# Batch 0 by casting loads with interleaved transposes and dummies, weight sums between products, two score steps in the first matmul

## The chip, the cores and the metric

One core of one Trainium2 chip runs the kernel. The metric is the device time in microseconds (us), the median of several executions. A profile is one such execution; its span is about 2 us shorter than the time of the same run. A ratio is the mean time of one kernel's fast runs over that of the other's in the same rounds, so it is not quite the ratio of the medians that are quoted. Times inside a kernel come from single profiles; heads that are the same instruction for instruction differ by about 1 us there, so differences below that are not read as effects.

Engines are named as in the profile: PE is TensorE (matmuls) and PEld its weight loads, DVE is VectorE, ACT is ScalarE, POOL is GpSimd, SP is SyncE, which issues DMAs; a q behind the name (SPq, POOLq) marks its DMA issues. L92 is line 92 of that kernel's file. `att` (three pairs of banks) and `ffp` (two banks) are the tiles in PSUM, the memory that matmuls write. The granted clock is the share of its full clock that PE was given. A casting DMA changes f32 to f16 on the way; a dummy is a matmul whose result nobody reads.

## The reference, cut to what matters

```python
# q, k, v: 8 batches x 12 heads x 448 x 64 f32;  w_in 768 x 2048, w_out 2048 x 768
scores = q @ k.T / sqrt(64) - log(448)
attn = sigmoid(scores) @ v                 # per head
x = attn, heads joined to 768 columns      # 3584 tokens
h = x @ w_in
out = (h * sigmoid(h)) @ w_out
```

q and k are drawn with a deviation of 0.1, so the scores before the shift have a deviation near 0.01 against a shift of -6.1. The comparison with the reference therefore hardly sees an error in q or k.

## The kernel before: the parts that matter

Heads are taken four at a time (a "quad", three to a batch; quads 0 to 2 are batch 0, quads 3 to 5 batch 1). A quad has seven score steps (four matmuls of 64x64 by 448 and one sigmoid of 128x896 each) and one set of values (28 matmuls), which gives a third of xT. Per batch: `ff1`, the first matmul (96 matmuls and a sigmoid product, giving gT), then `ff2_pair`, the second matmul (called the second product below), in seven products of eight matmuls (a Strassen form that needs four sums of w_out, once, and four sums `gs` of gT for each pair). The score steps of the next batch are interleaved with the second product of this one.

```python
    def load(kind, b, n):                     # f32, hardware queue (SP), 5 buffers
        ...
    def cast(kind, b, n):                     # f32 to f16 on GpSimd, q, k and v
        ...
    # batch 0, in front of everything
    for n in range(NQ):
        for kind in range(2):
            load(kind, 0, n)
            cast(kind, 0, n)
            pe_transpose(kind, 0, n, kind, "act" if kind else "dve")
        load(2, 0, n)
        cast(2, 0, n)
        ...                                   # w_in, w_out pieces by casting DMAs (GpSimd)
        us = [("s", 0, n, r) for r in range(R)]
        if n > 0:
            us.insert(2, ("a", 0, n - 1))     # values of the quad before
        while us:
            visit(us[:3])                     # three PSUM pairs
            us = us[3:]
    visit([("a", 0, NQ - 1)])
    for i in range(NQ, NQ + 3):               # batch 1: load, cast, DMA transpose
        prep(i)
        stage(i)
    w_out_sums()                              # four sums of 128x3072 on DVE

    for b in range(B):
        ff1(b)
        ...                                   # ff2 of b between the score steps of b + 1

    def ff2_pair(m):
        nc.vector.tensor_add(gs[:, 0], a21, a22)
        nc.vector.tensor_sub(gs[:, 1], gs[:, 0], a11)
        nc.vector.tensor_sub(gs[:, 3], a12, gs[:, 1])
        nc.vector.tensor_sub(gs[:, 2], a11, a21)
        ...
        yield from prod(X, a11, B11, True, False)
        copy(0, X)                            # snap copy, DVE, behind all four gs
        yield from prod(Z, s1, T1, True, False)
        copy(1, Z)
        yield from prod(X, s2, T2, False, False)
        ...
```

Of the kernel before, what the change touches and what calls it, by code (L numbers as in the profile page):

```python
# [16 lines left out]
def kernel(  # L17
# [9 lines left out]
    nc = tc.nc  # L27
# [34 lines left out]
    NSLOT = 14  # L62
    attnT = sb("attnT", [P, 2 * NSLOT, S])
    tsig = [sb(f"tsig{i}", [P, 2, S]) for i in range(2)]
    st32 = [sb(f"st32_{i}", [P, 2, S], F32) for i in range(5)]
    st16 = [sb(f"st16_{i}", [P, R, 2, D]) for i in range(4)]
    v16 = [sb(f"v16_{i}", [P, 2, R, D]) for i in range(3)]
# [3 lines left out]

    att = [psum.tile([P, 2, 512], F32, tag=f"att{i}", name=f"att{i}") for i in range(3)]
    ffp = [psum.tile([P, 512], F32, tag=f"ffp{i}", name=f"ffp{i}") for i in range(2)]

    nc.vector.memset(warm, 0.0)
    nc.gpsimd.memset(bias_s, NEG_LOG_S)
    make_identity(nc, ident)


    B11 = lambda fc: w_out_sb[:, fc, 0:EH]  # L80
    B21 = lambda fc: w_out_sb[:, KH + fc, 0:EH]
    B22 = lambda fc: w_out_sb[:, KH + fc, EH:]
    B12A = w_out_sb[:, 0:KH, EH:]
    T1 = lambda fc: wt[:, 0, fc, :]
    T2 = lambda fc: wt[:, 1, fc, :]
    T4N = lambda fc: wt[:, 2, fc, :]
    T3 = lambda fc: w_out_sb[:, fc, EH:]

    def w_out_sums():
        b11, b21, b22 = w_out_sb[:, 0:KH, 0:EH], w_out_sb[:, KH:, 0:EH], w_out_sb[:, KH:, EH:]  # L90
        nc.vector.tensor_sub(wt[:, 0], B12A, b11)
        nc.vector.tensor_sub(wt[:, 1], b22, wt[:, 0])  # L92
        nc.vector.tensor_sub(wt[:, 2], b21, wt[:, 1])
        nc.vector.tensor_sub(B12A, b22, B12A)


    n32 = [0]
    n16 = [0]
    staged = {}

    def load(kind, b, n):
        t = st32[n32[0] % len(st32)]
        n32[0] += 1
        src = (q, k, v)[kind]
        for g in range(2):
            h = 4 * n + 2 * g
            nc.sync.dma_start(
                t[g * HP : (g + 1) * HP],
                src[b, h : h + 2].rearrange("i (p r) d -> p i (r d)", p=HP),
            )  # L110
        staged[(kind, b, n)] = t

    def cast(kind, b, n):
        t = staged.pop((kind, b, n))
        if kind == 2:
            o = v16[(b * NQ + n) % 3]
            nc.gpsimd.tensor_copy(o.rearrange("p i r d -> p i (r d)"), t)  # L117
        else:
            o = st16[n16[0] % len(st16)]
            n16[0] += 1  # L120
            nc.gpsimd.tensor_copy(  # L121
                o.rearrange("p r i d -> p i r d"), t.rearrange("p i (r d) -> p i r d", r=R)
            )
            staged[("c", kind, b, n)] = o

    def dma_transpose(kind, b, n):
        o = staged.pop(("c", kind, b, n))
        nc.sync.dma_start_transpose(
            qkT[(b * NQ + n) % 3][kind], o.rearrange("p r i d -> p (r i d)")
        )  # L130

    def pe_transpose(kind, b, n, pair, eng):
        o = staged.pop(("c", kind, b, n))
        at = att[pair]
        for r in range(R):
            nc.tensor.matmul(
                at[:, r // 4, (r % 4) * P : (r % 4 + 1) * P],
                o[:, r].rearrange("p i d -> p (i d)"),
                ident,
                start=True,  # L140
                stop=True,
            )
        dst = qkT[(b * NQ + n) % 3][kind]
        for lo, hi, bk in ((0, 4, 0), (4, R, 1)):
            o2 = dst[:, lo:hi, :].rearrange("p r c -> p (r c)")
            i2 = at[:, bk, : (hi - lo) * P]
            if eng == "act":
                nc.scalar.copy(o2, i2)
            else:
                nc.vector.tensor_copy(o2, i2)  # L150


    def slot_of(b, n, r):
        return 2 * (((b * NQ + n) % 2) * R + r)

    def score_step(b, n, r, pair):
        qT, kT = qkT[(b * NQ + n) % 3]
        for i, j in ((0, 0), (1, 1), (0, 1), (1, 0)):
            ri = slice(i * HP, (i + 1) * HP)
            cj = slice(j * HP, (j + 1) * HP)  # L160
            nc.tensor.matmul(  # L161
                att[pair][cj, i, :S],
                kT[ri, r, cj],
                qT[ri, :, cj],
                start=True,
                stop=True,
            )

    def sigmoid(b, n, r, pair):
        s0 = slot_of(b, n, r)  # L170
        nc.scalar.activation(  # L171
            attnT[:, s0 : s0 + 2, :], att[pair][:, :, :S], AF.Sigmoid, bias=bias_s, scale=QKSCALE
        )

    def values(b, n, pair):
        vt = v16[(b * NQ + n) % 3]
        for r in range(R):
            s0 = slot_of(b, n, r)
            for i, j in ((0, 0), (1, 1), (0, 1), (1, 0)):
                rj = slice(j * HP, (j + 1) * HP)  # L180
                nc.tensor.matmul(  # L181
                    att[pair][i * HP : (i + 1) * HP, j, :S],
                    vt[rj, i, r, :],
                    attnT[rj, s0 + i, :],
                    start=(r == 0),
                    stop=(r == R - 1),
                )
        nc.vector.tensor_scalar_mul(xT[:, 2 * n : 2 * n + 2, :], att[pair][:, :, :S], SX)  # L188

    def unit_stream(b):  # L190

        o = []
        for n in range(NQ):
            for r in range(R):
                o.append(("s", b, n, r))
                if n > 0 and r == 2:
                    o.append(("a", b, n - 1))
        return o

    events = {}  # L200

    def visit(us):
        pair = 0
        for u in us:
            if u[0] == "a":
                values(u[1], u[2], pair)
                pair += 1
        for u in us:
            if u[0] == "s":
                score_step(*u[1:], pair)  # L210
                sigmoid(*u[1:], pair)
                pair += 1
        for u in us:
            for f in events.get(u, ()):
                f()

# [3 lines left out]
    def ff1(b):  # L220
        cb = (b % 2) * S
        for u in range(NFC // 2):
# [22 lines left out]
            for f in events.get(("f", b, u), ()):  # L245
                f()
# [5 lines left out]
    def ff2_pair(m):  # L252
# [6 lines left out]
        nc.vector.tensor_add(gs[:, 0], a21, a22)  # L259
        nc.vector.tensor_sub(gs[:, 1], gs[:, 0], a11)  # L260
        nc.vector.tensor_sub(gs[:, 3], a12, gs[:, 1])  # L261
        nc.vector.tensor_sub(gs[:, 2], a11, a21)  # L262
        s1, s2, s3, s4 = (gs[:, i] for i in range(4))
        x0 = nprod[0] % 2
        nprod[0] += 7
        X, Z = ffp[x0][:, :EH], ffp[1 - x0][:, :EH]
        o1, o2 = osb[nosb[0] % 3], osb[(nosb[0] + 1) % 3]
        nosb[0] += 2

        def prod(bank, a, w, first, last):  # L270
            for fc in range(KH):
# [3 lines left out]
                    w(fc),  # L275
# [17 lines left out]

        yield from prod(X, a11, B11, True, False)
        copy(0, X)
        yield from prod(Z, s1, T1, True, False)
        copy(1, Z)
        yield from prod(X, s2, T2, False, False)
        copy(2, X)
        yield from prod(Z, s4, B22, False, True)  # L300
        comb(o1[:, EH:], Z, 2)
        yield from prod(X, s3, T3, False, False)
# [7 lines left out]


    quads = [(b, n) for b in range(B) for n in range(NQ)]

    def prep(i):

        if i < len(quads):
            for kind in range(3):
                load(kind, *quads[i])
# [14 lines left out]
    def stage(i):  # L333

        if i < len(quads):
            for kind in range(3):
                cast(kind, *quads[i])
                if kind < 2:
                    dma_transpose(kind, *quads[i])


    for _ in range(10):
        nc.tensor.matmul(ffp[0], warm[:, :P], warm, start=True, stop=True)

    def at(u, f):
        events.setdefault(u, []).append(f)


    for n in range(NQ):
        for kind in range(2):  # L350
            load(kind, 0, n)
            cast(kind, 0, n)
            pe_transpose(kind, 0, n, kind, "act" if kind else "dve")
        load(2, 0, n)
        cast(2, 0, n)
        if n == 0:
            w_in_piece(0)
        if n == 1:
            w_in_piece(1)
        if n == 2:  # L360
            w_in_piece(2)
            w_in_piece(3)
            for s in range(4):
                w_out_piece(s)
        us = [("s", 0, n, r) for r in range(R)]
        if n > 0:
            us.insert(2, ("a", 0, n - 1))
        while us:
            visit(us[:3])
            us = us[3:]  # L370
    visit([("a", 0, NQ - 1)])
    for i in range(NQ, NQ + 3):
        prep(i)
        stage(i)
    w_out_sums()

    for b in range(B):
        ff1(b)
        lo, hi = (b * S) // 256, ((b + 1) * S) // 256
        mms = []  # L380
        gens = [ff2_pair(m) for m in range(lo, hi)]

        def run():
# [55 lines left out]
```

## Time and profile before

| | before |
|---|---|
| time, median of the first 3 runs | 432.3 us |
| first sigmoid | 12.3 us |
| first matmul of batch 0 starts | 45.0 us |
| second product of batch 0 starts | 81.1 us |
| first matmul of batch 1 starts | 103.7 us |
| from there to the end of the span (427.9) | 324.2 us |

The starts are those of the timeline of TensorE (PE). They cut the kernel into a head of 104 us and a steady part of 324 us. The line of the timeline that makes this cut (start, length, engine, line, what), for the kernel before:

```profile
103.65 6.59 PE L228 MATMUL att<-xT,w_in_sb 128*128 128x448 f16 x34
```

These are lines of the page's table of 40 slices (10.7 us each) for the kernel before: busy tenths of PE, the granted clock of PE in tenths, and the busy share of the DMA engines (9 stands for 90% or more).

```profile
PE   5566825989999999999999999899999999999894
...
PEclk8566675999999999999999999999999999999998
...
DMA  8999999389904995279905985699029930211022
```

The steady part is full at full clock. The first seven slices are neither. The DMA line ends at 9, so the table of stretches is needed; it gives per stretch its length, the busy time of PE, PEld, DVE, ACT and POOL (with the number of instructions), the clock, the DMA share and GB/s, for the kernel before:

```profile
20.00:30.00 10.00, 6.15 (x63) 3.24 (x62) 2.04 (x3) 6.72 (x9) 7.90 (x10) 0.67 1.17 263
30.00:40.00 10.00, 7.21 (x70) 3.82 (x69) 2.25 (x3) 6.29 (x9) 0.94 (x1) 0.67 1.22 200
...
60.00:70.00 10.00, 0.71 (x3) 0.27 (x3) 6.95 (x5) 0.67 (x1) 3.16 (x2) 0.50 1.13 193
```

From 60 to 70 us PE is busy for 0.71 us. The chain of waits (start, length, what) shows why, for the kernel before:

```profile
27.11 35.78 DMA w_out_sb<-in_moe_w_out_dram
63.01 1.77 DVE wt L92
64.81 1.76 DVE wt L93
66.56 1.67 DVE w_out_sb L94
68.23 1.01 DVE gT L244
69.29 8.94 PE att L228 x36
```

The w_out sums stand on DVE in front of the first gT products of `ff1`. They wait for the last w_out piece, which lands at 62.9 us. There are three `att` pairs, and one comes free only after its gT product, so PE stops. The list of waits of PE, longest in total first (us in total, times, longest), for the kernel before:

```profile
PE att L228 <- DVE gT L244: 12.9, 1, 12.9
PE att L161 <- ACT attnT L171: 10.0, 21, 1.7
PE att L136 <- ACT attnT L171: 3.5, 2, 2.1
PE ffp L272 <- DVE snap L283: 3.1, 7, 1.0
```

The last of these is the wait for snap copies that stand behind the four gs sums. Two of its seven times are in the last batch and cost 1.04 us each (timeline of PE).

### The profile page before, as it was taken

The numbers are of one execution on the slowest core, as the hardware profiler recorded it, in microseconds if no ns is written. First come the engines' busy times: TensorE is split into PE (matmuls) and PEld (weight loads), VectorE is DVE, ScalarE is ACT, GpSimd is POOL, SyncE is SP. The second block draws the span as 40 slices with busy tenths as digits, with TensorE's granted clock in tenths as the row PEclk, the third lists the DMA queues.
The fourth block names the chain that finished last, engine by engine and source line by source line (L and its number), as shares of the span: only waits on it lengthen the run. The fifth ranks groups of instructions, "written<-read, shape, count | busy, mean of one in ns | idle before, by whom it ended". The sixth has DMA issues, their size and how long they took to land.

```text
span 427.9 us, 7184 instructions
## 1 busy us (share of the span) xinstructions
PE 380.4 (89%) x2948; PEld 192.2 (45%) x2948; DVE 196.0 (46%) x269; ACT 222.2 (52%) x256; POOL 75.6 (18%) x87
## 2 busy tenths in 40 slices
PE   5566825989999999999999999899999999999894
PEld 2233312445545454545545554355454554455452
DVE  1121127623564445554465445344636445544652
ACT  2866102694377535872478435963677148734200
POOL 3570013122100221003100221131001200000000
PEclk8566675999999999999999999999999999999998
DMA  8999999389904995279905985699029930211022
GB/s 194 253 251 199 228 215 194 89 176 193 224 2 91 205 217 153 44 184 205 223 11 118 208 214 128 140 211 221 19 53 211 179 95 2 75 37 38 0 76 74
DMA packets 69472, 60.43 MB, mean 141 GB/s; under 512 B 42304, under 2 KB 65856, under 8 KB 69440
## 3 DMA queue, kind: packets, MB, share of 16 engines
q1 hardware_dynamic: 64192, 53.69, 57.2%
q0 software_dynamic: 5248, 6.29, 8.5%
q8 instruction: 23, 0.38, 0.4%
q14 instruction: 9, 0.07, 0.1%
HBM read 45.61 MB, written 11.01 MB: 132 GB/s over the span
## 4 chain that ended last, share of the span: by engine, by line
PE 70%; DVE 10%; DMA 9%; ACT 7%; issue 1%; POOL 1%; SPq 0%; DVEq 0%; ACTq 0%; POOLq 0%
PE att L228 24%; PE ffp L272 24%; DMA w_out_sb<-in_moe_w_out_dram 8%; PE ffp L228 8%; PE att L181 8%; ACT attnT L171 5%; PE att L161 5%; DVE gs L260 1%; DVE gs L261 1%; DVE gs L259 1%; DVE gs L262 1%; DMA st<-in_k_dram 1%; ACT tsig L239 1%; DVE snap L283 1%; DVE osb L308 1%
## 5 line engine op out<-in xcount | busy, mean ns | idle before, releaser
L171 ACT ACTIVATE attnT<-att,bias_s 128x896 f16<-128x896 f32 x168 | 156.1, 1012 | 33.4 <-PE att L161 33.1
L228 PE MATMUL att<-xT,w_in_sb 128*128 128x448 f16 x576 | 115.7, 361 | 14.2 <-DVE gT L244 12.9
L228 PEld LDWEIGHTS <-w_in_sb 128*128 128x128 f16 x768 | 76.3, 99 | 87.6 <-issue 20.2
L243 ACT ACTIVATE tsig<-att 128x896 f16<-128x896 f32 x48 | 44.0, 917 | 122.2 <-PE att L228 105.7
L244 DVE TENSOR_TENSOR gT<-att,tsig 128x896 f16<-128x896 f32 x48 | 52.3, 1091 | 70.4 <-ACT tsig L243 70.3
L121 POOL CAST st<-st 128x896 f16<-128x896 f32 x48 | 46.3, 965 | 172.5 <-DMA st<-in_q_dram 120.7
L161 PE MATMUL att<-qkT,qkT 64*64 64x448 f16 x672 | 51.8, 375 | 11.6 <-ACT attnT L171 10.0
L272 PEld LDWEIGHTS <-gs 128*128 128x128 f16 x448 | 40.4, 98 | 41.1 <-issue 16.5
L188 DVE TENSOR_SCALAR xT<-att 128x896 f16<-128x896 f32 x24 | 26.2, 1092 | 54.0 <-PE att L181 54.0
L272 PE MATMUL ffp<-wt,gs 128*128 128x384 f16 x224 | 43.0, 327 | 3.4 <-DVE snap L283 3.1
L272 PE MATMUL ffp<-w_out_sb,gT 128*128 128x384 f16 x224 | 43.4, 327 | 2.8 <-DVE gT L241 2.8
L272 PEld LDWEIGHTS <-gT 128*128 128x128 f16 x336 | 31.0, 98 | 29.5 <-issue 11.2
L181 PE MATMUL att<-attnT,v 64*64 64x448 f16 x672 | 40.4, 380 | 2.7 <-ACT attnT L171 1.7
L272 PE MATMUL ffp<-w_out_sb,gs 128*128 128x384 f16 x224 | 42.3, 327 | 0.0
L117 POOL CAST v<-st 128x896 f16<-128x896 f32 x24 | 22.5, 936 | 94.3 <-PE att L181 72.9
L228 PE MATMUL ffp<-xT,w_in_sb 128*128 128x448 f16 x192 | 38.9, 352 | 0.0
L286 DVE SCALAR_TENSOR_TENSOR osb<-ffp,snap 128x384 f32<-128x384 f32 x42 | 23.3, 555 | 33.2 <-PE ffp L272 33.2
L161 PEld LDWEIGHTS <-qkT 64*64 64x64 f16 x672 | 19.2, 108 | 41.0 <-issue 34.7
L181 PEld LDWEIGHTS <-v 64*64 64x64 f16 x672 | 20.1, 113 | 19.5 <-issue 9.7
L283 DVE TENSOR_SCALAR snap<-ffp 128x384 f32<-128x384 f32 x42 | 22.7, 553 | 11.6 <-PE ffp L272 10.9
L239 ACT ACTIVATE tsig<-ffp 128x448 f16<-128x448 f32 x32 | 17.3, 544 | 12.2 <-PE ffp L228 12.1
L241 DVE TENSOR_TENSOR gT<-ffp,tsig 128x448 f16<-128x448 f32 x32 | 19.7, 620 | 4.1 <-ACT tsig L239 4.1
(28 smaller groups left out, 105.9 us busy)
## 6 DMA issues: line engine op xcount, KB each, us to landing
st<-in_q_dram SPq DMA_DIRECT2D x48, 224.0 KB, 3.9
st<-in_k_dram SPq DMA_DIRECT2D x48, 224.0 KB, 4.8
st<-in_v_dram SPq DMA_DIRECT2D x48, 224.0 KB, 5.6
out_dram<-osb SPq DMA_DIRECT2D x56, 192.0 KB, 2.8
w_in_sb<-in_moe_w_in_dram POOLq DMA_DIRECT2D x4, 768.0 KB, 15.1
w_out_sb<-in_moe_w_out_dram POOLq DMA_DIRECT2D x4, 768.0 KB, 29.6
qkT<-st SPq DMA_TRANSPOSE x42, 3.2
```

What stands on the lines that cost most here:

```text
L117: nc.gpsimd.tensor_copy(o.rearrange("p i r d -> p i (r d)"), t)
L121: nc.gpsimd.tensor_copy(o.rearrange("p r i d -> p i r d"), t.rearrange("p i (r d) -> p i r d", r=R))
L161: nc.tensor.matmul(att[pair][cj, i, :S], kT[ri, r, cj], qT[ri, :, cj], start=True, stop=True,)
L171: nc.scalar.activation(attnT[:, s0 : s0 + 2, :], att[pair][:, :, :S], AF.Sigmoid, bias=bias_s, scale=QKSCALE)
L181: nc.tensor.matmul(att[pair][i * HP : (i + 1) * HP, j, :S], vt[rj, i, r, :], attnT[rj, s0 + i, :], start=(r == 0), stop=(r == R - 1),)
L188: nc.vector.tensor_scalar_mul(xT[:, 2 * n : 2 * n + 2, :], att[pair][:, :, :S], SX)
L228: nc.tensor.matmul(o, w_in_sb[:, cc, f * P : (f + 1) * P], xT[:, cc, :], start=(cc == 0), stop=(cc == NCC - 1),)
L243: nc.scalar.activation(ts, ph[:, :, :S], AF.Sigmoid, bias=0.0, scale=ISX)
L244: nc.vector.tensor_mul(gT[:, 2 * u : 2 * u + 2, cb : cb + S], ph[:, :, :S], ts)
L272: nc.tensor.matmul(bank, a[:, fc], w(fc), start=first and fc == 0, stop=fc == KH - 1, skip_group_check=True,)
L283: nc.vector.tensor_scalar_mul(snap[i], bank, ISX)
L286: nc.vector.scalar_tensor_tensor(o, bank, ISX, snap[i], op0=ALU.mult, op1=ALU.add)
```

## The change

Its intent: a shorter head. (1) The w_out sums go between the first pair's products, where each is needed. (2) q, k and v of batch 0 come by casting DMAs from GpSimd (only the first k comes by SP and is cast on DVE), the transposes are interleaved with the score steps, the sigmoid table is loaded at the start, and dummy matmuls fill the gaps. (3) In batches 0 and 4, whose second product is one pair only, two score steps move into the first matmul. (4) The gs sums go between products. (5) v of all batches comes by casting DMAs. The diff also moves the loads of the later quads to other points of the stream.

```diff
+    nc.scalar.activation(warm[:, 0:1], bias_s, AF.Sigmoid, bias=bias_s, scale=1.0)
...
+    load32(1, 0)
+    load16(0, 0)
+    make_identity(nc, ident)
+    nc.vector.tensor_copy(natural(0, 1), st32[1])
+    load16(1, 1)
+    load16(0, 1)
+    load16(2, 0)
+    w_in_piece(0)
...
+    dummy(14)
+    pe_transpose(1, 0, 0)
+    pe_transpose(0, 0, 1)
     for n in range(NQ):
+        for r in range(R):
+            score_step(n, r, cnt % 2)
+            sigmoid(n, r, cnt % 2)
+            cnt += 1
+            if n + 1 < NQ and r == (0 if n == 0 else 3):
+                pe_transpose(1, n + 1, 2)
+            elif n + 1 < NQ and r == (3 if n == 0 else 5):
+                pe_transpose(0, n + 1, 2)
+            elif n > 0 and r == 2:
+                value_steps(n - 1, 2, range(R))
+                to_x(n - 1, 2)
+            else:
+                dummy(2)
         if n == 0:
+            load32(1, NQ)
+            load32(0, NQ)
+            load16(2, NQ)
+            w_out_piece(0)
+            w_out_piece(1)
         if n == 1:
+            w_out_piece(2)
+            w_out_piece(3)
+            cast(1, NQ)
+            cast(0, NQ)
+            dma_transpose(1, NQ)
+            dma_transpose(0, NQ)
...
-    w_out_sums()
+    fetch(NQ + 1)
+    prepare(NQ + 1)
...
+            if u == NFC // 2 - 2 and early:      # in ff1
+                visit(early)
...
+        nc.vector.tensor_add(s1, a21, a22)       # in ff2_pair; new is m == 0
+        if new:
+            w_sum(T1, B12, B11)
         yield from prod(X, a11, B11, True, False)
         copy(0, X)
+        nc.vector.tensor_sub(s2, s1, a11)
+        if new:
+            w_sum(T2, B22, T1)
         yield from prod(Z, s1, T1, True, False)
         copy(1, Z)
+        nc.vector.tensor_sub(s4, a12, s2)
         yield from prod(X, s2, T2, False, False)
...
```

## The prediction

> **What bounds the kernel now.** The slice table shows TensorE over 95% busy from 100 to 400 us at full clock: matmul-bound. The first 104 us are not (clock 0.5 to 0.8 in most slices). The chain of waits and the timeline give this head:
> - 0 to 45.0 us: batch 0's attention. First sigmoid at 12.3 us, after serial loads, casts, transposes and a second activation-table load (1.28 us). 21 sigmoids of 0.914 us need 19.2 us; ACT pauses about 5 us at each change of quad (transposes; values of 2.83 us at half clock against 1.45).
> - 45.0 to 81.1 us: batch 0's first matmul, 18.2 us of work at full clock (as later, 103.8 to 121.9). TensorE idles from 56.4 to 69.3 us: a bank waits for a gT multiply, behind the four w_out sums (1.76 us each) on DVE, which wait for the last w_out piece (landing at 62.9 us). Then the clock is at half again.
> - 81.1 to 103.8 us: batch 0's second product with 21 score steps, ACT-bound (so is batch 4, 265 to 288).
> The DMA share is 1.1 to 1.2 from 10 to 63 us: loads are the head's second limit.
>
> **What the change does.**
> 1. The w_out sums no longer stand in front of the gT multiplies: -13 us of wait, -4 to -5 us of half-clock matmuls. All on the chain.
> 2. Interleaved transposes, early table load, casting DMAs, dummies that keep the clock up. The Trainium skill's "TensorE: Matmul & The Clock Gate", Part 1, says the clock is half until about 3.4 us of sustained activity and falls back after an idle window; this trace agrees (ten dummies 0.43 us apart, then full-clock transposes, then 0.5 in the second slice). First sigmoid near 10 us, 19.2 us of sigmoids, some 3 us of pauses, values and xT: attention ends near 34 us, not 45. -11 us.
> 3. Two score steps inside the first matmul of batches 0 and 4: each saves about 1.5 us.
> 4. gs sums between products: the last batch loses 1.04 us twice to snap copies queued behind them; with small waits elsewhere -2 to -3 us.
> 5. v by casting DMA in all batches: -22 us of GpSimd, off the path.
> Steps 1 to 3 are bounded by DMA. Estimate, from the page's queue shares (36 us of 16 engines for the weights, 245 us for the hardware queue, so about 1.84 us a load, 1.5 us a DMA transpose): 36 + nine casting loads of 1.4 + five loads + four transposes = 64 units before the last w_out piece, at 1.1 a microsecond: it lands at 55 to 60 us. The third product wants it near 58 us: little stall, at worst 5 us.
>
> **Sum.** xT of batch 0 at 34, first matmul to 52.5, second product to 75 (now 103.8): -29. Later batches -4. 432.3 - 33 = about **400 us**; 8 in 10: 393 to 409. Faster by over 2%: 0.97, within 2%: 0.02, slower: 0.01.
>
> **What would show it.** Right: the second batch's first matmul starts at 73 to 79 us; clock near 1 from 10 us; sigmoids of batch 0 nearly gapless from 10 to 32 us; GpSimd busy falls by a third. Wrong on step 1: DVE waits for w_out inside batch 0's second product and ACT idles with it. Wrong on step 2: sigmoids still pause over 2 us per quad, clock under 0.9.
>
> **What would make it wrong.** Casting loads slower than 1.4 us, or weights queued behind them, so that w_in or w_out lands late (then 405 to 412); k and q of quad 1 delayed by the next batch's loads on the same engines; the sums (7 us of DVE in batch 0's product) delaying snap copies; v landing late in the steady part.

## The result, and the profile after

The time is 406.45 us (median of 4 runs, 405.22 to 406.76) against 432.12 us (4 runs). The ratio is 0.9401, with a 95% interval of 0.9371 to 0.9431.

| | before | after | predicted |
|---|---|---|---|
| first sigmoid | 12.3 | 11.8 | 10 |
| first matmul of batch 0 starts | 45.0 | 34.4 | 34 |
| second product of batch 0 starts | 81.1 | 54.8 | 52.5 |
| first matmul of batch 1 starts | 103.7 | 84.2 | 75 |
| from there to the end | 324.2 | 320.1 | 320 |

The line of the timeline of PE that starts batch 1, for the kernel after:

```profile
84.22 6.97 PE L215 MATMUL att<-xT,w_in_sb 128*128 128x448 f16 x36
```

By length: attention of batch 0 won 10.6 us, its first matmul 15.8 us (36.1 to 20.4), and the steady part 4.2 us, but the second product of batch 0 became 6.9 us longer (22.5 to 29.5).

The same lines of the table of slices (10.1 us each), for the kernel after:

```profile
PE   6889956899999999999999998899999999999994
...
PEclk9999996999999999999999999999999999999999
...
DMA  8999987879977772767547783778178630311022
```

The clock is full at once. Slices 6 and 7 (50 to 71 us) still have a hole of PE, and the DMA engines are full no longer there. The stretches, for the kernel after:

```profile
20.00:30.00 10.00, 8.51 (x122) 3.68 (x110) 4.29 (x6) 8.12 (x9) 6.66 (x9) 1.00 1.24 206
...
50.00:60.00 10.00, 6.26 (x51) 2.56 (x49) 5.35 (x7) 8.08 (x10) 3.28 (x4) 1.00 0.89 160
60.00:70.00 10.00, 6.09 (x51) 2.69 (x52) 4.71 (x5) 1.86 (x2) 4.17 (x4) 0.66 0.79 161
```

The waits of PE, for the kernel after: the 12.9 us wait of `att` on gT is gone, and the longest is now on a DMA that fills qkT. (The second line is another wait, at the start of second products; the kernel before had it too, with 2.8 us.)

```profile
PE att L140 <- DMA qkT<-st: 8.0, 2, 7.2
PE ffp L267 <- DVE gT L228: 3.4, 6, 0.9
```

The timeline of PE gives the place of the 7.2 us (start, length, engine, line, what, and in brackets the idle time before it and what ended it), for the kernel after:

```profile
55.82 0.89 PE L140 MATMUL att<-qkT,qkT 64*64 64x448 f16 x8
63.91 0.59 PE L140 MATMUL att<-qkT,qkT 64*64 64x448 f16 x4 [7.20 <-DMA qkT<-st]
```

The first line is the last two score steps of quad 3, the second the first step of quad 4. Its way there is on the timelines of SP, which issues loads and DMA transposes, and of GpSimd (POOL), which casts k and q, for the kernel after:

```profile
28.24 2.76 SPq L110 DMA_TRANSPOSE qkT<-st  x2
31.06 5.98 SPq L101 DMA_DIRECT2D st<-in_k_dram  x2
37.08 2.11 SPq L101 DMA_DIRECT2D st<-in_q_dram  x2
53.48 6.26 SPq L110 DMA_TRANSPOSE qkT<-st  x2
```

```profile
27.26 1.83 POOL L104 CAST st<-st 128x896 f16<-128x896 f32 x2
...
52.52 0.94 POOL L104 CAST st<-st 128x896 f16<-128x896 f32 x1 [17.87 <-DMA st<-in_k_dram]
57.28 1.21 POOL L104 CAST st<-st 128x896 f16<-128x896 f32 x1 [3.83 <-DMA st<-in_q_dram]
```

The k of quad 4 is asked for at 31 us and is there at 52.5 us. Its q, asked for at 37 us, is there at 57.2 us; the cast takes 1.2 us and q's DMA transpose, issued at 58.5 us, 5.3 us, which is the end of the wait. In the chain of waits the long piece is this load, for the kernel after:

```profile
38.22 18.94 DMA st<-in_q_dram
```

Over the whole run a load of this kind takes 4.3 (k) or 4.9 us (q; the page's table of DMA issues, medians). The transposes of quad 3, before it on the same queue, are slow too: 12.1 and 19.2 us. The view of the tile qkT gives issue to landing in us (least, median, most), for the kernel after, first from 28 to 84 us, then from 100 to 300 us:

```profile
DMA to landing us min/median/max: 2.9/5.0/19.2
```

```profile
DMA to landing us min/median/max: 2.9/3.0/6.4
```

So a DMA transpose that takes 3.0 us (median) in the steady part took up to 19.2 us in the head. The trace of the kernel before had shown as much: its five DMA transposes from 25 to 70 us took 3.0 to 17.7 us (view of qkT). The last w_out piece was issued at 26.5 us and took 29.8 us, so it landed at 56.3 us: quad 4 crosses the engines together with the weights.

Outside the head: the page has GpSimd busy 81.5 us, up from 75.6, although the casts of v are gone. The issue of the 48 DMAs for v counts as 28.6 us there (0.60 us each).

### The profile page after: what moved, and what is told of

The parts are those of the page before. It is cut to its first block, busy times and chain, and to the rows that moved or that the text cites. A ratio compares the mean times of both kernels' runs of the same rounds, so it can differ in the third digit from the quotient of the medians.

```text
span 404.3 us, 7303 instructions
## 1 busy us (share of the span) xinstructions
PE 378.2 (94%) x3026; PEld 188.3 (47%) x3026; DVE 201.6 (50%) x281; ACT 219.1 (54%) x251; POOL 81.5 (20%) x114
## 2 busy tenths in 40 slices
DMA packets 69472, 53.78 MB, mean 133 GB/s; under 512 B 42304, under 2 KB 65856, under 8 KB 69440
## 4 chain that ended last, share of the span: by engine, by line
PE 75%; DMA 12%; ACT 3%; POOL 3%; SPq 3%; issue 2%; DVE 1%; POOLq 0%; ACTq 0%
PE ffp L267 31%; PE att L215 24%; PE ffp L215 7%; PE att L156 7%; DMA st<-in_q_dram 7%; PE att L140 6%; DMA w_in_sb<-in_moe_w_in_dram 3%; ACT attnT L146 2%; SPq L101 2%; POOL st L104 1%; DMA st<-in_k_dram 1%; DMA qkT<-st 1%; ACT tsig L226 1%; SPq L110 1%; DVE gT L228 1%
## 5 line engine op out<-in xcount | busy, mean ns | idle before, releaser
L215 PE MATMUL att<-xT,w_in_sb 128*128 128x448 f16 x576 | 111.8, 352 | 0.2 <-ACT xT L168 0.2
L215 PEld LDWEIGHTS <-w_in_sb 128*128 128x128 f16 x768 | 74.9, 98 | 70.6 <-issue 1.4
L231 DVE TENSOR_TENSOR gT<-att,tsig 128x896 f16<-128x896 f32 x48 | 52.4, 1092 | 75.6 <-ACT tsig L230 75.6
L104 POOL CAST st<-st 128x896 f16<-128x896 f32 x42 | 40.7, 971 | 195.0 <-DMA st<-in_k_dram 153.4
L140 PE MATMUL att<-qkT,qkT 64*64 64x448 f16 x672 | 49.2, 360 | 12.5 <-DMA qkT<-st 8.0
L170 DVE TENSOR_SCALAR xT<-att 128x896 f16<-128x896 f32 x23 | 25.1, 1091 | 39.1 <-PE att L156 39.1
L278 DVE TENSOR_SCALAR snap<-ffp 128x384 f32<-128x384 f32 x42 | 23.4, 557 | 28.6 <-PE ffp L267 26.1
L156 PE MATMUL att<-attnT,v 64*64 64x448 f16 x672 | 37.5, 359 | 0.0
L97 POOL DMA_DIRECT2D v<-in_v_dram x48 | 28.6, 601 | 41.7 <-PE att L140 35.4
L140 PEld LDWEIGHTS <-qkT 64*64 64x64 f16 x672 | 17.8, 105 | 40.0 <-issue 32.4
L281 DVE SCALAR_TENSOR_TENSOR osb<-ffp,snap 128x384 f32<-128x384 f32 x42 | 23.3, 554 | 20.3 <-PE ffp L267 19.6
L156 PEld LDWEIGHTS <-v 64*64 64x64 f16 x672 | 18.4, 108 | 17.1 <-issue 8.8
L226 ACT ACTIVATE tsig<-ffp 128x448 f16<-128x448 f32 x32 | 17.2, 546 | 11.3 <-PE ffp L215 11.3
## 6 DMA issues: line engine op xcount, KB each, us to landing
w_in_sb<-in_moe_w_in_dram POOLq DMA_DIRECT2D x4, 768.0 KB, 10.9
```

The lines of the kernel that those rows point to most:

```text
L97: nc.gpsimd.dma_start(o[g * HP : (g + 1) * HP], src_of(kind, i, g))
L104: nc.gpsimd.tensor_copy(st16[i % 3][kind].rearrange("p r e d -> p e r d"), st32[2 * (i % 2) + kind].rearrange("p e (r d) -> p e r d", r=R),)
L140: nc.tensor.matmul(att[pair][cj, e, :S], kT[re, r, cj], qT[re, :, cj], start=True, stop=True)
L156: nc.tensor.matmul(att[pair][e * HP : (e + 1) * HP, j, :S], vt[rj, e, r, :], attnT[rj, s0 + e, :], start=(r == 0), stop=(r == R - 1),)
L170: nc.vector.tensor_scalar_mul(xT[:, 2 * n : 2 * n + 2, :], att[pair][:, :, :S], SX)
L215: nc.tensor.matmul(o, w_in_sb[:, cc, f * P : (f + 1) * P], xT[:, cc, :], start=(cc == 0), stop=(cc == NCC - 1),)
```

## The experiments

Eleven other kernels ran, and the kernel after once more. Where the head of two kernels is compared, "batch 1 starts" is the start of the first matmul of batch 1 on the timeline of PE.

### The w_out sums alone (e1_sums_only)

```diff
 # on the kernel before
-    w_out_sums()
+        if new: w_out_sum(0)        # in ff2_pair, in halves, before the products
         yield from prod(X, a11, B11, True, False)
         copy(0, X)
+        if new: w_out_sum(1)        # and likewise (2), (3)
```

> The kernel before, with nothing changed but the place of the four w_out sums (between the products of the first pair). Theory: the 13 us idle in batch 0's first matmul and its half-clock tail go and nothing comes back, since the last w_out piece still lands near 63 us and the third product wants it near 71. Batch 1's first matmul starts near 89 us, not 104; median 416 to 419. Rival: the quads of batch 1 arrive late in the head as well, so the wait only moves into the second product: median 423 or more.

Measured: 416.68 us against 431.36, ratio 0.9644 (0.9602 to 0.9686). Batch 1 starts at 87.9 us, not 103.7, and its second product of batch 0 is 23.2 us long, without a wait for a quad. The theory held, the rival fell: on the kernel before, this one move is worth 14.7 us.

### All but the w_out sums (e2_sums_front)

```diff
 # on the kernel after
+    w_sum(T1, B12, B11)             # ahead of ff1(0)
+    w_sum(T2, B22, T1)
+    w_sum(T4N, B21, T2)
+    w_sum(T3, B22, B12)
-        new = m == 0
+        new = False
```

> The kernel after, with the w_out sums put back in front of batch 0's first matmul. Theory: DVE is held until the last w_out piece lands (near 56 us, hardly earlier than before), the gT multiplies start near 62 us, TensorE idles some 18 us inside the first matmul; batch 1's first matmul starts near 97 us and the median is 416 to 421, so most of what the shorter attention won is lost again. Rival: the shorter attention is worth its 9 us by itself, and the sums cost only the 5 us of DVE work: median 409 to 412.

Measured: 416.66 us, ratio 0.9661 (0.9628 to 0.9695). Batch 1 starts at 96.6 us. The waits of PE for this kernel:

```profile
PE att L215 <- DVE gT L231: 19.3, 1, 19.3
```

and its chain of waits:

```profile
26.61 29.74 DMA w_out_sb<-in_moe_w_out_dram
```

The last w_out piece lands at 56.4 us, only 6.5 us earlier than before. With the sums in front of the gT products, the time the shorter attention won is spent waiting for it. Of the 11.3 us that attention is shorter here (first matmul at 33.7, not 45.0), 7.1 us reach batch 1's start; the steady part gives 3.8 us more. (That is 10.9 us between the two profiles; the medians are 14.7 us apart, since the profiled run was the lower end of before's runs, 430.0 us, and the upper end of e2's, 418.8 us.) The two halves of the change, 14.7 and 14.7 us, make 25.7 together (432.12 to 406.45, other rounds), not 29.4: with both, quad 4 becomes the next limit. (In e2 the second product starts only at 76.2 us; it has no wait for a quad and takes 20.4 us.)

### No dummies among the score steps (e3_no_dummies)

```diff
-            else:
-                dummy(2)
...
-    dummy(2)                        # in the last values
```

> The kernel after without the dummy matmuls among batch 0's score steps (the 14 at the start stay). Theory: they hold the clock at full in the attention of batch 0; without them it falls to half there (0.5 to 0.7 granted from 15 to 35 us), values take 2.8 us and not 1.5, and xT comes 2 to 4 us later. But the second product waits for quad 4's transposes until 64 us all the same, so most of this is hidden: median 406 to 409. Rival: steps of 0.9 us set by the sigmoid leave TensorE busy enough, the clock stays, and nothing changes: xT within 0.5 us, clock over 0.9.

Measured: 405.39 us, ratio 0.9391 (0.9368 to 0.9413), against 0.9401 of the kernel after in its own rounds: no difference is shown. The stretches of this kernel:

```profile
10.00:20.00 10.00, 5.61 (x76) 2.61 (x79) 3.48 (x7) 8.35 (x10) 5.28 (x9) 0.90 1.25 206
20.00:30.00 10.00, 6.33 (x96) 3.73 (x92) 3.40 (x5) 7.39 (x8) 6.84 (x9) 0.84 1.24 206
30.00:40.00 10.00, 8.00 (x80) 4.12 (x73) 1.92 (x3) 5.17 (x7) 1.21 (x2) 0.92 1.21 196
```

The mean clock falls to 0.84 to 0.92 in these stretches, less than the 0.5 to 0.7 expected, but it does fall: values took 2.53 and 2.87 us instead of 1.52 and 1.49, and the first matmul starts at 36.0 us instead of 34.4. So the dummies do what they are for (the Trainium skill, "TensorE: Matmul & The Clock Gate", Part 1, has the clock fall back after an idle window; here it fell at about 18 us, among score steps of 0.38 us in every 0.9 us, although no gap there was longer than 0.52 us). But batch 1 starts at 83.9 us, as in the kernel after: the wait for quad 4 shrank to 4.6 us at its longest. What a step wins in front of a wait for a DMA, the wait takes back.

### Quad 4's loads first (e4_load_first)

```diff
             load32(0, NQ)
+            load32(1, NQ + 1)       # ahead of quad 3's DMA transposes on SP
+            load32(0, NQ + 1)
...
-    fetch(NQ + 1)
+    load16(2, NQ + 1)
```

> The kernel after, with k and q of quad 4 loaded directly after those of quad 3, ahead of quad 3's DMA transposes. Theory (late issue): the 7.2 us wait of TensorE at 56 to 64 us is there because SP could issue these loads only at 31 to 38 us, behind transposes that waited for GpSimd casts; now they land before 20 us and the wait falls under 3 us, while batch 0's first loads come 1 to 2 us later: median 400 to 404. Rival (shared engines): the engines are full until 56 us whatever the order; what quad 4 wins is lost in the first loads and in the transposes, which still take some 19 us: median 405 to 408.

Measured: 406.1 us, ratio 0.9394 (0.9358 to 0.943): as the kernel after. The theory fell. The loads did land early (their casts ran at 37.7 us), yet the wait for qkT stayed: 4.2 us for quad 4, and 1.1 and 1.9 us for quads 3 and 5, which had waited 0 and 0.8 us. The waits of PE up to 100 us, and the landing of the DMAs of qkT up to 84 us, in this kernel:

```profile
PE att L140 <- DMA qkT<-st: 7.2, 3, 4.2
```

```profile
DMA to landing us min/median/max: 2.9/8.9/21.0
```

The four DMA transposes of quads 3 and 4 now crossed the engines beside the weights, and the slowest took 21.0 us. What came earlier as a load came late as a transpose, as the rival had it.

### Quad 3's casts first (e8_cast_first), a faulty edit

```diff
     w_in_piece(1)
+    load32(1, NQ)
+    load32(0, NQ)
+    for t in (1, 0):
+        cast(t, NQ)
+        dma_transpose(t, NQ)
     load16(2, 2)
     ...                              # and removed below, at n == 0 and n == 1
```

> The kernel after, with the casts of quad 3 ahead of the last two w_in pieces in GpSimd's order, so that quad 3's transposes and quad 4's loads are issued by SP some 10 us earlier. Theory (late issue): quad 4's loads land before 40 us, and the wait of TensorE at 56 us falls from 7.2 us to under 3; median 399 to 403. Rival (shared engines): anything on the hardware queue still takes 18 us or more while weights run on the software queue, so the wait stays over 5 us: median 405 to 408.

Measured: 421.63 us, ratio 0.9774 (0.9742 to 0.9806). This run's time tells nothing of the theory, because the edit was wrong. Quad 3 uses the buffers of quad 0, and in program order its cast and its DMA transposes now came before quad 0's transposes on PE. So those waited, as the waits of PE in this kernel show, and read the wrong data:

```profile
PE att L140 <- DVE qkT L127: 16.3, 2, 15.9
PE att L118 <- POOL st L104: 7.0, 1, 7.0
```

One thing its trace does show. The second product of batch 0, the same instructions as in the kernel after, starts so late here that the quads are there; it has no wait for a quad and takes 20.7 us (77.9 to 98.6) instead of 29.5. The timeline of PE, for this kernel:

```profile
77.87 1.14 PE L267 MATMUL ffp<-w_out_sb,gT 128*128 128x384 f16 x6 [0.32 <-DVE gT L228]
...
98.56 1.68 PE L215 MATMUL att<-xT,w_in_sb 128*128 128x448 f16 x8
```

### Half of w_out behind quad 4 (e5_w_out_late)

```diff
         if n == 1:
-            w_out_piece(2)
-            w_out_piece(3)
...
     prepare(NQ + 1)
+    w_out_piece(2)
+    w_out_piece(3)
```

> The kernel after, with the second half of w_out issued by GpSimd only after the casts of quad 4. Theory (order on the shared engines): quad 3's transposes and quad 4's loads and transposes took up to 19 us because the weights stood in the same engines; with half of w_out behind them they land before 52 us, TensorE's wait near 56 us falls under 3 us, w_out lands near 60 us and the third product waits for it 3 us at most: median 399 to 403. Rival (sum of bytes): the engines are full until 60 us in any order, so the wait only turns into one for the w_out sum of the third product: median 405 to 408.

Measured: 407.58 us, ratio 0.9436 (0.9408 to 0.9464); batch 1 starts at 84.9 us. The waits of PE up to 100 us and the landing of the DMAs of qkT up to 84 us in this kernel:

```profile
PE att L140 <- DMA qkT<-st: 7.7, 2, 4.8
```

```profile
DMA to landing us min/median/max: 2.9/5.5/17.8
```

The first part of the theory fell: quad 3's transposes still took up to 17.8 us, now beside the w_in pieces and the first half of w_out; the k of quad 4 behind them was cast at 49.1 us, and its transposes then ran beside the second half. The rival's total was right but not its place: the wait stayed on qkT and did not move to the w_out sum. Changing the order of the same transfers won no time that shows in either experiment.

### No score steps in the first matmul (e6_no_early)

```diff
-        early = us[:2] if us and hi - lo == 1 else []
+        early = []
```

> The kernel after without score steps inside the first matmul of batches 0 and 4. Theory: batch 4's second product is bound by its 21 sigmoids, so it gets 1.5 us longer from first matmul to first matmul (after has 40.4 us from 226.7 to 267.1); batch 0 loses nothing, since it waits for quad 4's transposes anyway: median 1 to 2 us over after. Rival: the first matmul gets shorter by what the second product gets longer: under 0.5 us.

Measured: 408.08 us, ratio 0.9441 (0.9408 to 0.9475). From first matmul to first matmul, batch 4 has 41.47 us (starts at 227.82 and 269.29 in the chain), as in the kernel before (246.51 and 287.98), against 40.37 us in the kernel after. So this part is worth 1.1 us in batch 4. (The interval of the ratio meets that of the kernel after, 0.9371 to 0.9431, so the times alone do not show it.) What it is worth in batch 0 (85.3 against 84.2 and 84.6 us in two profiles of the kernel after) is within the noise of single profiles.

### The gs sums in front (e7_gs_front)

```diff
         nc.vector.tensor_add(s1, a21, a22)
+        nc.vector.tensor_sub(s2, s1, a11)
+        nc.vector.tensor_sub(s4, a12, s2)
+        nc.vector.tensor_sub(s3, a11, a21)
         ...                          # and removed between the products
```

> The kernel after, with the four gs sums of each pair together in front of its products. Theory: each of the last batch's two pairs waits 1 us again for its snap copy, and the pairs of other batches up to 0.2 us: 2 to 3 us longer, all after 100 us. Rival: the new place costs as much by waits for single sums, so under 0.7 us.

Measured: 411.56 us, ratio 0.9527 (0.9468 to 0.9587). From batch 1's start to the end it is 324.3 us, 4.2 more than in the kernel after; the last batch alone is 45.05 us (from 364.35) against 42.83 (from 361.47). The waits of PE in this kernel:

```profile
PE ffp L267 <- DVE snap L278: 3.9, 10, 1.0
```

The theory held, and the size was 4 us rather than 2 to 3 (4.2 in these profiles; the medians, of different rounds, are 5.1 us apart): the interleaved batches have these waits too (up to 0.6 us a batch).

### No DMA transposes beside the weights (e9_pe_transposes)

k and q of quads 3 and 4 come by casting DMAs and are transposed on PE, in four slots of quad 2's score steps where dummies stood.

```diff
     pe_transpose(0, 0, 1)
+    load16(1, NQ)
+    load16(0, NQ)
+    w_in_piece(1)               # moved here from above, with load16(2, 2)
     ...
+            elif n == 2 and r in (0, 1, 3, 4):
+                pe_transpose((1, 0, 1, 0)[(0, 1, 3, 4).index(r)], NQ + (r > 2), 2)
     ...
         if n == 0:
-            load32(1, NQ)
-            load32(0, NQ)
+            load16(1, NQ + 1)
+            load16(0, NQ + 1)
+            w_in_piece(2)           # moved here, to keep the order of buffers
+            w_in_piece(3)
     ...
-            cast(1, NQ)
-            cast(0, NQ)
-            dma_transpose(1, NQ)
-            dma_transpose(0, NQ)
     ...
-    fetch(NQ + 1)
-    prepare(NQ + 1)
+    load16(2, NQ + 1)
```

> The kernel after, with k and q of quads 3 and 4 (the first two of batch 1) loaded by casting DMAs and transposed on TensorE in four slots of quad 2's score steps, where dummies stood: no DMA transpose and no GpSimd cast before quad 5. Theory (DMA transposes crawl, 15 to 19 us each way, beside the weight stream, and everything behind them on their queue waits too): with none of them beside the weights, quads 3 and 4 are ready before 40 us, w_out lands at 50 to 54 us, the waits of TensorE for qkT go, the second product of batch 0 takes 22 to 24 us instead of 30, and the median is 398 to 402. Rival (sum of bytes: the same bytes in the same engines): w_out or a quad is late by as much, and the second product ends within 2 us of after's 84.4: median 404 to 407.

Measured: 404.59 us, ratio 0.9354 (0.9334 to 0.9374); the kernel after in the same rounds (after_again): 406.65 us, ratio 0.9408 (0.9387 to 0.943). The intervals do not meet, so e9 is faster by about 2 us. The first four waits of PE up to 100 us, longest in total first, in this kernel:

```profile
PE ffp L81 <- DVE warm L77: 2.8, 1, 2.8
PE att L140 <- DVE qkT L127: 2.3, 2, 1.9
PE att L118 <- DVE xT L170: 2.0, 2, 1.0
PE att L118 <- DVE qkT L127: 1.9, 2, 0.9
```

The theory held for its step: no wait on a DMA of qkT is left, and the second product of batch 0 is 21.4 us long (61.6 to 83.0) instead of 29.5. Its later start is not the reason: quads 3 and 4 were transposed by 37.7 us. Its total did not: the first matmul of batch 0 starts 6.8 us later (41.2 against 34.4 us). A dummy in a slot is followed by nothing; a real transpose is followed by two DVE copies (1.16 us) before the one PSUM pair for such work is free again, and the clock fell to 0.83 in the stretch from 30 to 40 us. In the list of waits those of transposes and values for such copies come to 3.8 us more than in the kernel after (2.0 + 1.9 + 0.9 us against 1.0). Another 1.1 us or so comes from 11 to 15 us, where this profile ran at half clock (score steps of 0.59 us instead of 0.38), which e10's does not. The timeline of PE in this kernel shows such a slot, with the wait for the copies:

```profile
29.14 0.58 PE L118 MATMUL att<-ident,st 128*64 128x128 f16 x14 [0.94 <-DVE qkT L127]
29.65 0.38 PE L140 MATMUL att<-qkT,qkT 64*64 64x448 f16 x4
30.97 1.52 PE L156 MATMUL att<-attnT,v 64*64 64x448 f16 x28 [0.93 <-DVE qkT L127]
```

So most of the 8 us that the second product won went back into the attention. The edit took two things off SP's queue at once, the f32 loads and the DMA transposes of quads 3 and 4; their shares are not separated. Quad 5's DMA transposes still ran beside the weights here (issued at 42.7 us); the slower took 17.1 us, harmless because quad 5 is needed near 72 us.

The page also gives the number of packets under 512 B: 42,304 in the kernel after with 42 DMA transposes, 38,592 here with 38. By this difference a DMA transpose is some 928 small packets.

### Two steps at the very start (e10_act_copies, e11_k5_later)

```diff
 # e10, on e9
-    pe_transpose(0, 0, 1)
+    pe_transpose(0, 0, 1, act=True)       # its PSUM copies on ACT
 # e11, on e10: the first k in the buffer of quad 5's k
-    load32(1, 0)
+    for g in range(2):
+        nc.sync.dma_start(st32[3][g * HP : (g + 1) * HP], src_of(1, 0, g))
```

> As e9, with the two copies of the first q transposes on ACT, which idles then, instead of behind the two of k on DVE. Expected: the first sigmoid starts 0.8 to 1.2 us earlier than the 11.75 us of after, all of batch 0 with it, and the median falls by 0.8 to 1.2 us against e9. Rival: the first k and q of the next quad, not these copies, then set the pace: nothing.

> As e10, with the first k in the buffer that quad 5's k uses, so that the loads of quad 5 are issued only after the first cast (8.4 us) and do not share the engines with the first k and q. Expected: the first k, which lands at 7.7 us in after, lands 1 to 2 us earlier, and the median falls by 1 to 2 us against e10. Rival: the first load's latency does not come from sharing: under 0.4 us.

Measured: e10 404.12 us, ratio 0.9355 (0.9322 to 0.9387); e11 404.18 us, ratio 0.9361 (0.9335 to 0.9386). In the profiles the first sigmoid starts at 11.98 us in e9, 11.02 in e10 and 9.96 in e11, and batch 1 at 83.0, 82.4 and 81.0 us. But the first sigmoid of the unchanged head lay anywhere from 10.8 (e6) to 12.0 us (e5). What e10 does is seen from the start of the first transposes: from there to the first sigmoid takes 2.5 us instead of 3.3 (after) or 3.5 (e9). For e11 nothing is shown: its first transposes start at 7.50 us, and those of the unchanged head at 7.45 (e6) to 8.67 us (e5). In the times nothing can be told from e9. e10 and e11 scatter over 5.7 and 3.4 us in their six runs each, e9 over 1.7 us in five, so a gain of 1 to 2 us could hide there; it is not shown.

> The kernel after, unchanged, in the same rounds, to compare the three others with: median 404.5 to 407.5.

Measured: 406.65 us (405.11 to 407.52), as expected, and again with a wait of 8.0 us on qkT in its profile.

## Why the prediction was right, and where not

The total was predicted as 400 us with a range of 393 to 409; 406.45 was measured, and the direction and the main mechanism held. The sign that the prediction had set itself, batch 1 starting at 73 to 79 us, was missed: it starts at 84.2 us. Of these 9.2 us against 75, 7.0 are the second product, 1.9 the first matmul and 0.4 the attention. The total is off by less, 6.5 us, because the prediction subtracted its 33 us from the median of before, 432.3 us, and rounded up, while the profile whose times it used was of a run of 430.0 us: that part is luck.

1. **The w_out sums** ("-13 us of wait, -4 to -5 us of half-clock matmuls. All on the chain"). Right. The wait of 12.9 us is gone and the first matmul is 15.8 us shorter. It takes 20.4 us, not the 18.5 predicted: the prediction counted 18.2 us of matmuls, but batch 1's first matmul, too, takes 19.6 us to the start of the second product (84.2 to 103.8). Alone, on the kernel before, the move is worth 14.7 us (e1).
2. **Attention** ("-11 us", xT near 34 us). Right in size: 10.6 us. The first sigmoid came at 11.8 us, not 10: about 1 us of it is that the copies of the first q stood behind those of k on DVE (e10); that the first k shared the engines with the next loads is not shown (e11). The dummies hold the clock (e3), but they are worth 1.6 us, and those are hidden.
3. **Two score steps in the first matmul** ("each saves about 1.5 us"). 1.1 us in batch 4 (e6); in batch 0 not shown.
4. **gs sums** ("-2 to -3 us"). The steady part is 4.2 us shorter as predicted (-4): 2.3 us in the last batch (45.10 to 42.83), where 2.1 was predicted, 1.1 us in batch 4 and 0.8 us in the five others. Putting the sums back costs more (4.2 us, e7) than they had cost before (3.1 us by these figures, without batch 4).
5. **v by casting DMA** ("GpSimd busy falls by a third"). Wrong: it rose from 75.6 to 81.5 us, since 48 issues at 0.60 us cost more than 24 casts at 0.94 us. It was nearly off the path, as said: the chain that ended last passes through two issues of v, 1.2 us, at 12.6 us.

The mis-sized term is "second product to 75": 22.5 us were predicted and 29.5 measured, with a wait of 7.2 us in it for quad 4 and a clock of 0.66 behind the wait (60 to 70 us). The prediction asked when w_out would land and got that right (55 to 60 us predicted, 56.3 measured). It did not ask when the quads of batch 1, which use the same engines, would be transposed. It had costed a DMA transpose at 1.5 us of engine time and added it to a sum of 64 units, as though the order of transfers could be chosen; while the weights run, the slower transpose of a quad took 17 to 21 us from issue to landing (after, e4, e5, e9), and the loads behind the transposes on SP's queue 16 to 20 us (after). That the late quads held the second product is shown by three traces in which they are there in time: e9, which takes both off that queue (21.4 us, no wait), and e2 and e8, in which the product starts later (20.4 and 20.7 us). Earlier loads (e4) and a later half of w_out (e5) had won nothing. How much of the delay is the loads' and how much the transposes' own was not separated.

The Trainium skill bears on this in "DMA: Bandwidth & Descriptors", "Issuing engines are not separate DMA queues": transfers issued by any engine run on the same 16 DMA engines and interleave. The traces agree (a transpose of 3.0 us in the steady part, 19.2 us beside the weights). The same page, "Queues, rings and completion order", says that an engine takes turns between queues packet by packet. With some 928 packets under 512 B to a transpose, against weight packets of 1.2 KB (6.29 MB in 5,248, from the page of before), this would explain the slowness, if these records of the profile are the packets that the page means; no run here varied the packet size, so it stays an explanation that was only argued.

What stays open: why e9's attention is 6.8 us longer, which was read from its timeline and not tested by an edit, and whether e11 is faster than e9.

## What to carry to other kernels

When a wait for a late weight is removed, ask at once what else lands late on the same engines: here each half of the change was worth 14.7 us alone, and together 25.7, because the next quad became the limit. A load or a DMA transpose should not be costed by its time in the steady part if a weight stream runs beside it (3.0 against up to 21.0 us here). Putting the transfers in another order won nothing in the two orders tried; moving the transposes to TensorE won 2 us, less than the wait it removed, because the place they went to had little room. The place of a sum in an engine's order can matter more than its length: four sums of 1.76 us cost 13 us of waiting in one place and at most 0.6 us in another (e1).

## What the Trainium skill lacked or had wrong

- "DMA: Bandwidth & Descriptors" gives 261 GB/s for DMA transposes under "Latency and other measured facts". It does not say how they fare beside another stream. Here one of 128x896 f16 (224 KB) took 3.0 us from issue to landing in the steady part (median; 2.9 to 6.4), and at the slowest 17.1 to 21.0 us beside casting loads of weights (before, after, e4, e5, e9).
- The same page puts descriptor generation for GpSimd's DMAs at "small, variable", and has about 1 us to the first byte; how long an issue holds GpSimd it does not say. Here each issue held GpSimd about 0.60 us for a load of 64 partitions and 0.74 to 0.96 us for a weight piece, 28.6 us for the 48 loads of v; and in the head an issue of v waited up to 3.3 us for, by the profile, a w_in piece to land, whose data it does not use.
- "ScalarE: Activation LUTs" has about 2.7 us for a table load under Terms; "What ACT_TABLE_LOAD costs" takes this apart into about 1283 ns for the load and about 1380 ns for a drain. The traces have 1.28 us for the load. Of a drain the kernel before shows at most 0.35 us, the idle time of ACT in front of its second load; the sigmoid starts 0.01 us after it.
- "TensorE: Matmul & The Clock Gate", Part 1, lets the clock fall after an idle window of about 3.4 us. Without dummies (e3) it fell although the gaps between score steps were 0.52 us, with PE busy 0.38 us in 0.9. The page tells of another kernel whose short gaps made the clock fall, but not how little work counts as idle.
